# Two decode layers with a resident ring: 64 more places of keys kept between layers, longer loads for heads 27 to 30, W2's last 64 rows loaded apart

## The chip, the cores and the metric

The kernel runs on one core of one Trainium2 chip. The metric is the device time of one execution in microseconds; the median of a kernel's runs is compared.

## What is computed

One token is decoded through two layers that share all weights and caches. Attention has 32 heads over a cache of 8192 keys and values of 128 numbers each, all in float32; then comes a block with a ReLU between two products.

```python
def _A_ref(x, k_cache, v_cache, wq, wo):      # B, Sq = 1, 1; D = 640; H, Dh = 32, 128; Sk = 8192
    q = (x @ wq).reshape(B, Sq, H, Dh).transpose(0, 2, 1, 3)
    scores = jnp.einsum("bhqd,bhkd->bhqk", q, k_cache) * (Dh ** -0.5)
    p = _softmax(scores, axis=-1)
    o = jnp.einsum("bhqk,bhkd->bhqd", p, v_cache)
    return o.transpose(0, 2, 1, 3).reshape(B, Sq, H * Dh) @ wo
...
x = x + _A_ref(_layernorm(x, axis=-1), A_k_cache, A_v_cache, A_wq, A_wo)
x = x + _B_ref(_layernorm(x, axis=-1), B_w1, B_w2)      # relu(x @ w1) @ w2, Dff = 1728
x = x + _A_ref(_layernorm(x, axis=-1), A_k_cache, A_v_cache, A_wq, A_wo)
x = x + _B_ref(_layernorm(x, axis=-1), B_w1, B_w2)
```

A head's keys are 4 MB and its values 4 MB, so a layer's caches are 256 MB, far more than fits beside the engines. Nearly all of the time is the reading of these.

## The kernel before

**The ring.** One SBUF tile, `ring`, takes the caches as they stream in. It is counted in places: one place is 8 numbers on each of 128 partitions, 4096 B. It has `RING` = 4760 places, `KEPT` = 3960 and 800 more. A head's keys take 1024 places, and so do its values. `UNITS` says in which blocks a head lies in DRAM; heads up to 26 are one block of keys and values (the host lays the caches out in the order of use, each block as 128 long rows), heads 27 to 31 are cut finer. A piece of keys is (row group, first column, columns); n columns of keys take n/2 places. A piece of values is (block, first row, rows).

**Two layers, one pass back.** Layer 0 walks heads 0 to 31, layer 1 walks them backwards, since both use the same cache. The last units of layer 0, those of heads 29 to 31 from `DROPPED` on, stay in the ring, `KEPT` places in all, and layer 1 doesn't load them again. Two units of head 30 go to the tiles `wct` and `mix` for layer 1 (`load_beside`, L227).

**What sets the order of loads.** `todo` is a fixed list of loads for the whole program. `pump` (L207) takes from its head: it looks for free places in one run (`place`, L181, for loads without a fixed place; a fixed one for heads 2 to 26, in slots of 256 places) and issues the load on SP's queue (L221); where there is no room it stops, and nothing behind it in the list is issued. `release` frees the places of a piece when PE's matmuls on it are written, and calls `pump` again. So on the chip SP waits for PE's use of a piece, then issues the load that takes its place. At the end of a layer four loads of W2 (12 blocks of 640 numbers) go to the 800 places behind `KEPT` and to what PE has freed.

**Beside it.** ScalarE's queue issues the loads of Wq and Wo in pairs (`load_pair`, L271), of W1 (L797), of W2's last two blocks (`w2_rest`, L799: 128 x 1280 numbers, in the tile `w_t`; of the second block only 64 rows are not zero) and of a piece of the weights for `mixing` (L802). `due` (L783) starts these by the head that is worked on.

**One head.** `scores` (L494) multiplies the keys in the ring by a spread-out query on PE (L499). DVE takes the maxima (L510), ScalarE the exponentials (L524), DVE transposes (L528), and `values` (L548) multiplies the values in the ring (L554). `output` brings the parts together. The two columns of a head's state for the softmax lie in the tile `h_t`, its sum in `sums`. The queries of four heads are computed ahead by a generator that PE and DVE work off in turns; `queries_by_halves` yields between DVE's write of `q_row` (L433) and PE's matmuls on it (L439), so that PE may do other work there. `mixing` uses the constant `ident`, a 128 x 128 identity that POOL makes once at the start. The program works on constants, Wq, Wo and the ring in SBUF; `dynamic_dma_scratch_size` reserves more of it.

Of the kernel before, what the change touches and what calls it, by code (L numbers as in the profile page):

```python
# [43 lines left out]
PARTS = {(0, 0): [4, 9], (1, 26): [4, 8], (1, 25): [4, 8], (1, 2): [4, 8], (1, 1): [2, 4, 6, 8], (1, 0): [2, 4, 6, 7, 8, 9]}  # L44
# [19 lines left out]
DROPPED = {29: 9, 30: 2}  # L64
KEPT = 3960
# [40 lines left out]
def decode_kernel(ctx: ExitStack, tc: tile.TileContext, x, kv, wqo, w1, w2, w2_rest, out):  # L106
# [16 lines left out]
    apart = {(29, 9): (3800, KEPT), (30, 0): (4464, 4544), (30, 1): (4544, RING), (30, 2): (3072, 3800)}  # L123
# [3 lines left out]
    def all_of(layer, u):  # L127
        todo.append((layer, u, 0, len(UNITS[u[0]][u[1]][1]), None))
# [8 lines left out]
    def turning(layer, heads, slot):  # L137

        for h in heads:
            for a, end in parts_of(layer, h):  # L140
                while a < end:
                    b = min(end, a + SLOTS - slot)
                    todo.append((layer, (h, 0), a, b, SLOT * slot))
                    slot = (slot + b - a) % SLOTS
                    a = b

    def anywhere(layer, h):
        for a, b in parts_of(layer, h):
            todo.append((layer, (h, 0), a, b, None))
# [22 lines left out]
    for us, dram in ((order, kv), (W2_ALL, w2)):
        o = 0
        for u in us:
            n = 8 * P * size(UNITS[u[0]][u[1]])
            source[u] = dram[o : o + n].rearrange("(p m) -> p m", p=P)
            o += n
# [29 lines left out]
    def pump():  # L207
        while todo:
            layer, u, first, last, at = todo[0]
            unit = UNITS[u[0]][u[1]]  # L210
            ns = [wide(kind_of(unit, t), piece) for t, piece in enumerate(unit[1])]
            n = sum(ns[first:last])
            if at is None:
                at = place(layer, u, n)
# [5 lines left out]
            o = 8 * sum(ns[:first])  # L220
            nc.sync.dma_start(ring[:, 8 * at : 8 * (at + n)], source[u][:, o : o + 8 * n])  # L221
            for t in range(first, last):
                live[layer, u, t] = at, ns[t]
                at_of[layer, u, t] = ring, 8 * at
                at += ns[t]

    def load_beside(where, at, n):  # L227
# [3 lines left out]
        nc.sync.dma_start(where[:, at : at + n], source[u])  # L231
# [136 lines left out]
    def deviations(xt, s):  # L368
# [4 lines left out]
        xc = work.tile([P, 2 * DH], F32, name="q_row")[:, :DR]  # L373
# [22 lines left out]
    def queries(g, xc, r):  # L396
# [12 lines left out]
        row = work.tile([P, 2 * DH], F32, name="q_row")[:, :DH]  # L409
# [8 lines left out]
    def queries_by_halves(g, xc, r):  # L418
# [696 lines left out]
```

## Time and profile before

| | |
|---|---|
| median of 3 runs | 1349.29 us (1348.77 to 1350.27) |
| profiled execution, its own time | 1349.0 us |
| its span | 1347.2 us |
| PE busy | 797.8 us (59%) |
| DVE busy | 248.3 us (18%) |
| ScalarE busy | 58.5 us (4%) |
| POOL busy | 2.9 us |
| read from HBM | 573.65 MB, 426 GB/s over the span |

The span is what the profiler's records cover; 1.8 us of the execution's own time lie around it. The lines below name L-numbers of the kernel before. A DMA's name reads destination<-source; `SPq` and `ACTq` are the queues that SyncE and ScalarE issue. "PE ps L499 <- DMA ring<-in_kv" is a wait of PE for a load of the ring.

### The profile page before, as it was taken

The numbers are of one execution on the slowest core, as the hardware profiler recorded it, in microseconds if no ns is written. First come the engines' busy times: TensorE is split into PE (matmuls) and PEld (weight loads), VectorE is DVE, ScalarE is ACT, GpSimd is POOL, SyncE is SP. The second block draws the span as 40 slices with busy tenths as digits, with TensorE's granted clock in tenths as the row PEclk, the third lists the DMA queues.
The fourth block names the chain that finished last, engine by engine and source line by source line (L and its number), as shares of the span: only waits on it lengthen the run. The fifth ranks groups of instructions, "written<-read, shape, count | busy, mean of one in ns | idle before, by whom it ended". The sixth has DMA issues, their size and how long they took to land.

```text
span 1347.2 us, 13344 instructions
## 1 busy us (share of the span) xinstructions
PE 797.8 (59%) x5966; PEld 261.2 (19%) x5966; DVE 248.3 (18%) x774; ACT 58.5 (4%) x149; POOL 2.9 (0%) x10
## 2 busy tenths in 40 slices
PE   3564445563655664667688754455466654656667
PEld 1121111111211211112252211112121111211214
DVE  1121111121212121112122211122111121111212
ACT  0000000000000000000000000000000000000000
POOL 0000000000000000000000000000000000000000
PEclk9688777778977886788798777898778788878889
DMA  9999999999999999999999999999999999999997
GB/s 413 429 427 437 430 439 428 438 420 428 442 434 422 441 427 423 446 419 419 425 385 425 435 432 436 424 441 429 437 430 430 424 437 436 434 419 438 424 426 326
DMA packets 22673, 574.52 MB, mean 426 GB/s; under 512 B 2516, under 2 KB 2648, under 8 KB 5464
## 3 DMA queue, kind: packets, MB, share of 16 engines
q1 hardware_dynamic: 19592, 529.84, 91.6%
q10 hardware_dynamic: 3024, 43.83, 7.7%
q8 instruction: 47, 0.77, 0.2%
q14 instruction: 10, 0.08, 0.0%
HBM read 573.65 MB, written 0.00 MB: 426 GB/s over the span
## 4 chain that ended last, share of the span: by engine, by line
DMA 65%; PE 26%; DVE 5%; ACT 1%; issue 1%; another core or an unknown queue 1%; ACTq 0%; SPq 0%; DVEq 0%
DMA ring<-in_kv 65%; PE ps L499 13%; PE outs L554 7%; DVE h_t L510 2%; ACT p L524 1%; DVE pt L528 1%; PE pm L515 1%; PE acc L468 1%; PE px L424 1%; DVE p L591 1%; PE px L456 0%; PE px L675 0%; DMA ring<-in_w 0%; DVE pT L530 0%
## 5 line engine op out<-in xcount | busy, mean ns | idle before, releaser
L499 PE MATMUL ps<-ring,spread_q 128*32 128x512 f32 (+3 forms) x2104 | 324.3, 765 | 312.2 <-DMA ring<-in_kv 307.3
L554 PE MATMUL outs<-ring,pT 128*4 128x512 f32 (+1 forms) x2032 | 258.9, 648 | 48.4 <-DVE pT L530 24.4
L499 PEld LDWEIGHTS ps<-ring,spread_q 128*32 128x32 f32 x2104 | 78.2, 137 | 493.2 <-issue 338.5
L510 DVE TENSOR_REDUCE h_t<-ps 128x1 f32<-128x512 f32 x64 | 44.3, 692 | 611.1 <-PE ps L499 611.1
L524 ACT ACTIVATE p<-ps,h_t 128x512 f32<-128x512 f32 x64 | 44.0, 687 | 1223.2 <-DVE h_t L522 1223.2
L554 PEld LDWEIGHTS outs<-ring,pT 128*4 128x4 f32 x2032 | 51.3, 91 | 211.0 <-issue 172.8
L601 PE MATMUL pm<-ones,p 128*128 128x1 f32 x120 | 22.9, 260 | 95.0 <-DVE p L591 95.0
L587 DVE TENSOR_SCALAR p<-outs,ind 128x128 f32<-128x128 f32 x60 | 21.1, 351 | 269.0 <-PE outs L554 269.0
L591 DVE SCALAR_TENSOR_TENSOR p<-outs,ind,p 128x128 f32<-128x128 f32 x180 | 63.1, 351 | 6.4
L528 DVE STREAM_TRANSPOSE pt<-p 128x512 f32<-128x512 f32 x64 | 46.5, 727 | 58.4 <-ACT p L524 58.4
L515 PE MATMUL pm<-row_of,h_t 128*128 128x16 f32 x128 | 26.3, 281 | 49.6 <-DVE h_t L510 48.9
L601 PEld LDWEIGHTS pm<-ones,p 128*128 128x128 f32 x120 | 17.8, 188 | 151.5 <-DVE p L591 150.2
L515 PEld LDWEIGHTS pm<-row_of,h_t 128*128 128x128 f32 x128 | 20.0, 196 | 109.8 <-DVE h_t L510 108.0
L675 PE MATMUL px<-w_t,wct 128*128 128x448 f32 (+1 forms) x80 | 36.7, 574 | 1.0 <-ACT wct L668 1.0
L424 PE MATMUL px<-pair,ln_xc 128*32 128x256 f32 x280 | 34.6, 396 | 4.4 <-ACT mix L683 4.4
L468 PE MATMUL acc<-pair,o_cols 128*32 128x320 f32 x224 | 36.2, 469 | 0.0
L424 PEld LDWEIGHTS px<-pair,ln_xc 128*32 128x32 f32 x280 | 15.7, 113 | 21.4 <-ACT mix L683 8.5
L522 DVE TENSOR_REDUCE h_t<-pm 128x1 f32<-128x16 f32 x64 | 11.2, 175 | 33.0 <-PE pm L515 33.0
L468 PEld LDWEIGHTS acc<-pair,o_cols 128*32 128x32 f32 x224 | 12.9, 117 | 16.8 <-issue 15.7
L675 PEld LDWEIGHTS px<-w_t,wct 128*128 128x128 f32 x80 | 13.8, 197 | 10.8 <-issue 9.3
L530 DVE COPY pT<-pt 128x64 f32<-128x64 f32 x64 | 14.4, 224 | 2.2
L605 DVE COPY o_cols<-pm 128x1 f32<-128x1 f32 x56 | 8.9, 159 | 28.4 <-PE pm L601 28.4
(130 smaller groups left out, 212.1 us busy)
## 6 DMA issues: line engine op xcount, KB each, us to landing
ring<-in_kv SPq DMA_DIRECT2D x24, 4096.0 KB, 31.1
ring<-in_kv SPq DMA_DIRECT2D x11, 6144.0 KB, 36.1
ring<-in_kv SPq DMA_DIRECT2D x31, 2048.0 KB, 35.1
pair<-in_wqo ACTq DMA_DIRECT2D x13, 2560.0 KB, 25.8
ring<-in_kv SPq DMA_DIRECT2D x14, 1024.0 KB, 15.1
ring<-in_w SPq DMA_DIRECT2D x4, 1280.0 KB, 25.9
w_t<-in_w ACTq DMA_DIRECT2D x1, 4320.0 KB, 27.5
pair<-in_wqo ACTq DMA_DIRECT2D x3, 1280.0 KB, 13.1
```

Source lines behind the costliest of these rows:

```text
L424: nc.tensor.matmul(pq[32 * j : 32 * j + 32, :n], xc[:, c : c + 1].to_broadcast([P, 32]), wq_t[g][:, c, j * n : (j + 1) * n], start=(c == 0 ...
L468: nc.tensor.matmul(acc[32 * half : 32 * half + 32, : 2 * DR], col.to_broadcast([P, 32]), wt[:, 2 * half * DR : 2 * (half + 1) * DR], start ...
L499: nc.tensor.matmul(hd.ps[32 * g : 32 * g + 32, c : c + n], spread_q[:, 3 - r : 35 - r], tile_of[:, at + g * n : at + (g + 1) * n], start=f ...
L510: nc.vector.tensor_reduce(hd.nm, hd.ps, AX.X, ALU.max, negate=True)
L515: nc.tensor.matmul(pt[:, :16], hd.nm.to_broadcast([P, P]), row_of.rearrange("p g r -> p (g r)"), start=True, stop=True,)
L524: nc.scalar.activation(hd.p, hd.ps, AF.Exp, bias=hd.low, scale=1.0, accum_out=hd.l)
L528: nc.vector.transpose(pt, hd.p)
L554: nc.tensor.matmul(hd.out[32 * g : 32 * g + 4, r : r + m].rearrange("p r d -> p (r d)"), hd.pT[:, 4 * i : 4 * i + 4], tile_of[:, v : v + m ...
L587: nc.vector.tensor_scalar(oc[:, 0], hd.out[:, 0], ind[:, :1], 0.0, op0=ALU.mult, op1=ALU.add)
L591: nc.vector.scalar_tensor_tensor(oc[:, r], hd.out[:, r], ind[:, r : r + 1], oc[:, r - 1], op0=ALU.mult, op1=ALU.add,)
L601: nc.tensor.matmul(pt[:, :1], oc[:, 3], ones, start=True, stop=True)
L675: nc.tensor.matmul(pt[:, :n], wct[:, c], w1_t[:, c, f : f + n], start=(c == 0), stop=(c == NB - 1),)
```

## The change

- **Kept keys.** `KEPT` goes from 3960 to 4024: of head 29's keys 448 columns of the last row group are kept, not 320. Layer 1 loads 64 places less.
- **Room for them.** DMA scratch goes from 1024 to 16. `ident` moves into the ring, behind the slots, so that `make_identity` runs again in layer 1 at the tenth head. The row of `queries_by_halves` moves to the tile "p", and the `yield` between its write and PE's matmuls goes, so `q_row` shrinks. `h_t` goes into `sums`; `ones`, `mhalf`, `ind` and `sel` become one tile; `m_s` shares a tile with `ln_m`.
- **Longer loads.** An entry of `todo` may now join several units (`ENDS` for layer 0, `STARTS` for layer 1), and the units of a head lie in one block in DRAM, so that a load may run over them. SP has 118 DMAs instead of 137: 11 ring loads fewer in layer 0 and 8 fewer in layer 1.
- **W2's rest.** `w2_rest` holds one block (128 x 640). The 64 rows of the second come by eight loads of 8 rows x 640 (`w2_last`), on ScalarE's queue, one at each of the heads 16 to 23 of layer 0; load i goes to every fourth partition from `LAST_AT[i]`.

```diff
-PARTS = {(0, 0): [4, 9], (1, 26): [4, 8], (1, 25): [4, 8], (1, 2): [4, 8], (1, 1): [2, 4, 6, 8], (1, 0): [2, 4, 6, 7, 8, 9]}
+PARTS = {(0, 0): [4, 9], (1, 26): [4, 8], (1, 25): [4, 8], (1, 2): [4, 8], (1, 1): [4, 8], (1, 0): [2, 4, 6, 7, 8, 9]}
...
 UNITS[29] = [
     ("k", K_ALL[:1]),
     ("k", K_ALL[1:2]),
     ("k", [(2, 0, 256)]),
-    ("k", [(2, 256, 256), (3, 128, 64)]),
+    ("k", [(2, 256, 256), (3, 0, 64)]),
     ("v", V_ALL[:1]),
     ("v", V_ALL[1:2]),
-    ("k", [(3, 0, 128)]),
     ("v", V_ALL[2:3]),
     ("v", V_ALL[3:]),
-    ("k", [(3, 192, 320)]),
+    ("k", [(3, 64, 448)]),
...
-DROPPED = {29: 9, 30: 2}
-KEPT = 3960
+DROPPED = {29: 8, 30: 2}
+ROWS = [[(h, i) for i in range(len(UNITS[h]))] for h in range(29)]
+ROWS += [[(h, i) for i in range(len(UNITS[h]))] for h in (29, 30, 31)]
+ENDS = [
+    [(27, 0), (27, 1)],
+    [(28, 0), (28, 1)],
+    [(28, 2), (28, 3)],
+    ROWS[29][:4],
+    [(29, 8)],
+    ROWS[29][4:8],
+    [(30, 0), (30, 1)],
+    [(30, 2)],
+    [(30, 3)],
+    [(30, 4)],
+] + [[u] for u in ROWS[31]]
+STARTS = [
+    [(29, 0)],
+    [(29, 1)],
+    [(29, 2)],
+    [(29, 3)],
+    ROWS[29][4:8],
+    ROWS[28][:3],
+    [(28, 3)],
+    [(27, 0)],
+    [(27, 1)],
+]
+KEPT = 4024
...
+LAST_AT = [32 * half + i for half in range(2) for i in range(4)]
...
-    apart = {(29, 9): (3800, KEPT), (30, 0): (4464, 4544), (30, 1): (4544, RING), (30, 2): (3072, 3800)}
+    apart = {(29, 8): (3800, KEPT), (30, 0): (RING - 296, RING), (30, 2): (3072, 3800)}
...
-    def all_of(layer, u):
-        todo.append((layer, u, 0, len(UNITS[u[0]][u[1]][1]), None))
+    def all_of(layer, us):
+        todo.append((layer, [(u, t) for u in us for t in range(len(UNITS[u[0]][u[1]][1]))], None))
...
-    for h in range(FULL[-1] + 1, H):
-        for i in range(len(UNITS[h])):
-            all_of(0, (h, i))
-    for u in W2_ALL:
-        all_of(0, u)
-    for h in range(H)[:FULL[-1]:-1]:
-        if h != 30:
-            for i in range(len(UNITS[h])):
-                if (h, i) not in kept:
-                    all_of(1, (h, i))
+    for us in ENDS + [[u] for u in W2_ALL]:
+        all_of(0, us)
+    for us in STARTS:
+        all_of(1, us)
...
-            layer, u, first, last, at = todo[0]
-            unit = UNITS[u[0]][u[1]]
-            ns = [wide(kind_of(unit, t), piece) for t, piece in enumerate(unit[1])]
-            n = sum(ns[first:last])
+            layer, pieces, at = todo[0]
+            ns = []
+            for u, t in pieces:
+                unit = UNITS[u[0]][u[1]]
+                ns.append(wide(kind_of(unit, t), unit[1][t]))
+            n = sum(ns)
             if at is None:
-                at = place(layer, u, n)
+                at = place(layer, pieces[0][0], n)
                 if at is None:
                     return
             elif not is_free(at, n):
                 return
             todo.pop(0)
-            o = 8 * sum(ns[:first])
-            nc.sync.dma_start(ring[:, 8 * at : 8 * (at + n)], source[u][:, o : o + 8 * n])
-            for t in range(first, last):
-                live[layer, u, t] = at, ns[t]
+            u, t = pieces[0]
+            block, o = source[u]
+            unit = UNITS[u[0]][u[1]]
+            o += 8 * sum(wide(kind_of(unit, i), unit[1][i]) for i in range(t))
+            nc.sync.dma_start(ring[:, 8 * at : 8 * (at + n)], block[:, o : o + 8 * n])
+            for (u, t), m in zip(pieces, ns):
+                live[layer, u, t] = at, m
                 at_of[layer, u, t] = ring, 8 * at
-                at += ns[t]
+                at += m
...
+    small = consts.tile([P, 12], F32, name="small")
+    ones, mhalf, ind, sel = small[:, 0:1], small[:, 1:2], small[:, 2:7], small[:, 7:12]
...
-    ident = consts.tile([P, P], F32, name="ident")
+    ident = ring[:, 8 * SLOT * SLOTS : 8 * SLOT * SLOTS + P]
     make_identity(nc, ident)
...
-        row = work.tile([P, n], F32, name="q_row")
+        row = work.tile([P, RUN], F32, name="p")[:, :n]
         nc.vector.tensor_scalar(
             row[:64], pq[:64, :n], r[0][:64], SCALE, op0=ALU.mult, op1=ALU.mult
         )
-        yield "pe"
         pt = ps_m.tile([P, 512], F32, name="px")
...
         def __init__(self, h, sums, j):
             self.h = h
             self.ps = ps_s.tile([P, RUN], F32, name="ps")
-            t = work.tile([P, 4], F32, name="h_t", bufs=2)
-            self.nm, self.low = (t[:, i : i + 1] for i in range(2))
-            self.sums = sums
-            self.l, self.rl = sums[:, j : j + 1], sums[:, HG + j : HG + j + 1]
+            self.l, self.rl, self.nm, self.low = (
+                sums[:, HG * i + j : HG * i + j + 1] for i in range(4)
+            )
...
             if L == 0 and where == 4:
                 nc.scalar.dma_start(w1_t, w1)
             if L == 0 and where == 7:
-                nc.scalar.dma_start(w2_t, w2_rest)
+                nc.scalar.dma_start(w2_t[:, 0], w2_rest)
+            if L == 0 and 16 <= where < 24:
+                a = LAST_AT[where - 16]
+                nc.scalar.dma_start(w2_t[a : a + 32 : 4, 1], w2_last[where - 16])
             if where == 8:
                 of, nth = divmod(last, HG)
                 nc.scalar.dma_start(
                     mix[:, :D], wqo[chain(of, 1)][:, of, nth * D : (nth + 1) * D]
                 )
+            if L and where == 9:
+                make_identity(nc, ident)
             if where == 11:
                 slow.append([mixing(), "dve"])
...
-        "w2_rest": rows[:, 4 * F_TILES :],
+        "w2_rest": rows[:, 4 * F_TILES],
+        "w2_last": np.stack([rows[a : a + 32 : 4, 4 * F_TILES + 1] for a in LAST_AT]),
...
-        "TRN2", target_bir_lowering=False, num_devices=1, dynamic_dma_scratch_size=1024
+        "TRN2", target_bir_lowering=False, num_devices=1, dynamic_dma_scratch_size=16
```

The loads that SP issues at the end of layer 0, from heads 25 and 26 (one load each) to head 29 (a row's size is partitions x numbers; a head's keys or values are 8192 numbers), before:

```order
L221 DMA ring<-in_kv 128x16384 x2
L221 DMA ring<-in_kv 128x8192 x2
L221 DMA ring<-in_kv 128x4096 x4
L221 DMA ring<-in_kv 128x2048 x2
L221 DMA ring<-in_kv 128x1024
L221 DMA ring<-in_kv 128x1280
L221 DMA ring<-in_kv 128x2048 x2
L221 DMA ring<-in_kv 128x512
L221 DMA ring<-in_kv 128x2048 x2
L221 DMA ring<-in_kv 128x1280
```

And now, from the same place, up to the first loads of head 30:

```order
L253 DMA ring<-in_kv 128x16384 x3
L253 DMA ring<-in_kv 128x8192 x2
L253 DMA ring<-in_kv 128x6400
L253 DMA ring<-in_kv 128x1792
L253 DMA ring<-in_kv 128x8192
L253 DMA ring<-in_kv 128x2368
L253 DMA ring<-in_kv 128x5824
```

Head 27 is one load instead of two, head 28 two instead of four, head 29 three instead of ten (its kept keys, 1792, ahead of its values), and head 30's first two units one.

The loads that SP issues at the start of layer 1, behind those to `wct` and `mix` (the first are head 29's keys and values, then come heads 28 and 27), before:

```order
L231 DMA mix<-in_kv 128x1728
L221 DMA ring<-in_kv 128x2048 x2
L221 DMA ring<-in_kv 128x1024
L221 DMA ring<-in_kv 128x1280
L221 DMA ring<-in_kv 128x2048 x2
L221 DMA ring<-in_kv 128x512
L221 DMA ring<-in_kv 128x2048 x2
L221 DMA ring<-in_kv 128x4096 x4
L221 DMA ring<-in_kv 128x8192 x6
```

And now:

```order
L264 DMA mix<-in_kv 128x1728
L253 DMA ring<-in_kv 128x2048 x2
L253 DMA ring<-in_kv 128x1024
L253 DMA ring<-in_kv 128x1280
L253 DMA ring<-in_kv 128x8192
L253 DMA ring<-in_kv 128x12288
L253 DMA ring<-in_kv 128x4096
L253 DMA ring<-in_kv 128x8192 x6
```

Head 29's values are one load of 1024 places where they were four of 256, the 512 of keys are gone since they are kept, and head 28 is two loads instead of four.

## Rows read from the trace of the kernel before

**Rows 1.** The page: DMA busy share in tenths and GB/s, 40 slices.

```profile
DMA  9999999999999999999999999999999999999997
GB/s 413 429 427 437 430 439 428 438 420 428 442 434 422 441 427 423 446 419 419 425 385 425 435 432 436 424 441 429 437 430 430 424 437 436 434 419 438 424 426 326
```

**Rows 2.** The page: chain that ended last, share of the span by engine.

```profile
DMA 65%; PE 26%; DVE 5%; ACT 1%; issue 1%; another core or an unknown queue 1%; ACTq 0%; SPq 0%; DVEq 0%
```

**Rows 3.** Waits: who for whom: us in all, count, mean us.

```profile
ACT p L524 <- DVE h_t L522: 1223.2, 64, 41.1
...
PE ps L499 <- DMA ring<-in_kv: 307.3, 48, 18.9
...
PEld px L439 <- DVE q_row L433: 8.3, 8, 1.1
```

**Rows 4.** Timeline of SP at the boundary: start us, us, queue, line, load.

```profile
676.22 0.33 SPq L221 DMA_DIRECT2D ring<-in_w  x1
...
702.30 0.33 SPq L221 DMA_DIRECT2D ring<-in_kv  x1
...
711.08 0.33 SPq L221 DMA_DIRECT2D ring<-in_kv  x1
```

**Rows 5.** Issues at 676.22, 702.30 and 166.52: KB, us to landing.

```profile
ring<-in_w SPq DMA_DIRECT2D x1, 640.0 KB, 22.6
...
ring<-in_kv SPq DMA_DIRECT2D x1, 640.0 KB, 13.6
...
w_t<-in_w_rest ACTq DMA_DIRECT2D x1, 640.0 KB, 24.7
```

**Rows 6.** Windows at both layers' ends: busy by engine, PEclk, DMA share, GB/s.

```profile
694.00:696.00 2.00, 1.90 (x30) 1.29 (x30) 0.97 (x5) 0.37 (x2) 0.00 (x0) 1.00 0.53 225
696.50:697.50 1.00, 1.00 (x34) 0.98 (x37) 0.22 (x2) 0.00 (x0) 0.00 (x0) 1.00 0.41 169
1338.00:1340.00 2.00, 2.00 (x56) 1.66 (x57) 0.53 (x4) 0.00 (x0) 0.00 (x0) 1.00 0.57 238
```

**Rows 7.** The page, DMA queues: packets, MB, share of 16 engines' span.

```profile
q1 hardware_dynamic: 19592, 529.84, 91.6%
...
q8 instruction: 47, 0.77, 0.2%
```

**Rows 8.** Windows of two stretches without idle DMA: columns as in rows 6.

```profile
40.00:600.00 560.00, 310.09 (x2070) 93.76 (x2074) 95.58 (x282) 22.82 (x58) 0.00 (x0) 0.79 1.00 432
610.00:660.00 50.00, 31.57 (x218) 9.90 (x222) 9.62 (x31) 2.33 (x6) 0.00 (x0) 0.76 1.01 423
```

**Rows 9.** DMA packets of 40 to 600, 610 to 660, and from 1344 on.

```profile
DMA packets 6501, 241.64 MB, mean 432 GB/s; under 512 B 720, under 2 KB 720, under 8 KB 976
...
DMA packets 2513, 21.14 MB, mean 423 GB/s; under 512 B 278, under 2 KB 278, under 8 KB 1046
...
DMA packets 8, 0.00 MB, mean 1 GB/s; under 512 B 4, under 2 KB 8, under 8 KB 8
```

**Rows 10.** Timeline: two issues of loads, W2's rest and the output.

```profile
166.52 0.34 ACTq L799 DMA_DIRECT2D w_t<-in_w_rest  x1
...
1344.59 0.66 SPq L1030 DMA_DIRECT2D out<-xr  x1
```

**Rows 11.** Groups by line: POOL's identity: count, busy us, mean ns.

```profile
masks.py:199 POOL TENSOR_SCALAR_AFFINE_SELECT ident<-ident 128x128 f32<-128x128 f32 x1 | 0.3, 292 | 0.1
masks.py:197 POOL MEMSET ident<- 128x128 f32 x1 | 0.2, 204 | 0.3 <-POOLq L1097 0.3
```

**Rows 12.** Chain of waits in time, at the boundary: start us, us, work.

```profile
696.55 4.90 DMA ring<-in_w
...
707.43 3.71 PE ps L499 x32
```

More of the change, by code (lines that the diff above doesn't have):

```diff
@@ L105, in decode_kernel @@
 @with_exitstack
-def decode_kernel(ctx: ExitStack, tc: tile.TileContext, x, kv, wqo, w1, w2, w2_rest, out):
+def decode_kernel(ctx: ExitStack, tc: tile.TileContext, x, kv, wqo, w1, w2, w2_rest, w2_last, out):
     nc = tc.nc
@@ L142, in turning @@
                     b = min(end, a + SLOTS - slot)
-                    todo.append((layer, (h, 0), a, b, SLOT * slot))
+                    todo.append((layer, [((h, 0), t) for t in range(a, b)], SLOT * slot))
                     slot = (slot + b - a) % SLOTS
@@ L148, in anywhere @@
         for a, b in parts_of(layer, h):
-            todo.append((layer, (h, 0), a, b, None))
+            todo.append((layer, [((h, 0), t) for t in range(a, b)], None))
     for h in range(FULL[0]):
@@ L169, in decode_kernel @@
     for u in W2_ALL:
-        all_of(1, u)
+        all_of(1, [u])
     source = {}
[L172 to L177, printed above, removed]
+    o = 0
+    for row in ROWS:
+        n = 8 * sum(size(UNITS[h][i]) for h, i in row)
+        block = kv[o : o + P * n].rearrange("(p m) -> p m", p=P)
+        o += P * n
+        a = 0
+        for h, i in row:
+            source[h, i] = block, a
+            a += 8 * size(UNITS[h][i])
+    o = 0
+    for u in W2_ALL:
+        n = 8 * P * size(UNITS[u[0]][u[1]])
+        source[u] = w2[o : o + n].rearrange("(p m) -> p m", p=P), 0
+        o += n
     live = {}
@@ L230, in load_beside @@
         assert 8 * size(UNITS[u[0]][u[1]]) == n
-        nc.sync.dma_start(where[:, at : at + n], source[u])
+        block, o = source[u]
+        nc.sync.dma_start(where[:, at : at + n], block[:, o : o + n])
         for t, piece in enumerate(pieces):
@@ L288, in decode_kernel @@
     pump()
-    ones = consts.tile([P, 1], F32, name="ones")
+    small = consts.tile([P, 12], F32, name="small")
+    ones, mhalf, ind, sel = small[:, 0:1], small[:, 1:2], small[:, 2:7], small[:, 7:12]
     nc.vector.memset(ones, 1.0)
-    sel = consts.tile([P, 5], F32, name="sel")
     nc.vector.memset(sel, 0.0)
@@ L372, in deviations @@
         nc.vector.tensor_scalar(m, pt[:, :1], 1.0 / D, 0.0, op0=ALU.mult, op1=ALU.add)
-        xc = work.tile([P, 2 * DH], F32, name="q_row")[:, :DR]
+        xc = work.tile([P, DR], F32, name="q_row")
         nc.vector.tensor_scalar(xc, xt, m, 0.0, op0=ALU.subtract, op1=ALU.add)
@@ L408, in queries @@
         yield "dve"
-        row = work.tile([P, 2 * DH], F32, name="q_row")[:, :DH]
+        row = work.tile([P, DR], F32, name="q_row")[:, :DH]
         nc.vector.tensor_scalar(row, pq[:, :DH], r[0], SCALE, op0=ALU.mult, op1=ALU.mult)
@@ L545, in totals @@
         nc.tensor.matmul(pt[:, :HG], ind[:, 4:5].to_broadcast([P, P]), sums[:, :HG], start=True, stop=True)
-        nc.vector.reciprocal(sums[:, HG:], pt[:, :HG])
+        nc.vector.reciprocal(sums[:, HG : 2 * HG], pt[:, :HG])
     def values(hd, piece, where, first, last):
@@ L645, in mixing @@
         wc = mix[:, :D]
-        s = work.tile([P, 1], F32, name="m_s")
+        s = work.tile([P, 1], F32, name="ln_m")
         nc.vector.tensor_reduce(s, wc, AX.X, ALU.add)
@@ L788, in due @@
                 o_cols[k] = work.tile([P, HG], F32, name="o_cols", bufs=2)
-                sums[k] = work.tile([P, 2 * HG], F32, name="sums", bufs=2)
+                sums[k] = work.tile([P, 4 * HG], F32, name="sums", bufs=2)
             if where and j == 0:
@@ L886, in attention_and_mlp @@
                 if k < NG - 1 and j == HG - 1:
-                    nc.vector.tensor_tensor(o_cols[k], o_cols[k], sums[k][:, HG:], op=ALU.mult)
+                    nc.vector.tensor_tensor(o_cols[k], o_cols[k], sums[k][:, HG : 2 * HG], op=ALU.mult)
         hd = opened(H - 1)
@@ L919, in attention_and_mlp @@
                 sums_of_rows(pt, rows, False)
-        o_late = work.tile([P, 2 * DH], F32, name="q_row")[:, :DH]
+        o_late = work.tile([P, DR], F32, name="q_row")[:, :DH]
         nc.vector.tensor_copy(o_late, late)
@@ L1056, in _laid_out @@
     o = 0
-    for h in range(H):
-        for unit in UNITS[h]:
-            n = 8 * size(unit)
-            block = kv[o : o + P * n].reshape(P, n)
-            o += P * n
-            a = 0
+    for row in ROWS:
+        n = 8 * sum(size(UNITS[h][i]) for h, i in row)
+        block = kv[o : o + P * n].reshape(P, n)
+        o += P * n
+        a = 0
+        for h, i in row:
+            unit = UNITS[h][i]
             for t, piece in enumerate(unit[1]):
```

2 lines of the change are left out of this document (removed).

## The prediction, made before the changed kernel ran

> **What bounds the kernel now.** I read the slices first: the DMA engines stand at 9 in 39 of 40 slices and move 413 to 446 GB/s, except in the slice that holds the layer boundary (385) and in the last (326) [rows 1]. The chain of waits gives 65% of the span to DMA [rows 2]. PE waits 307.3 us for ring loads in 48 waits, and ScalarE 1223.2 us for DVE, so neither is short of time [rows 3]. The queue of loads is the bound: what it no longer carries comes off the end, unless it runs dry, and what an engine off that path gets or loses costs nothing.
>
> Not all 16 DMA engines are equally late. The last W2 load of layer 0 is issued at 676.22 and lands after 22.6 us, at 698.8, but from 694 to 696 the DMA share is already 0.53, and 0.41 from 696.5 to 697.5: about half of the engines have run out while the others work on [rows 4 to 6]. Layer 1 ends alike, with 0.57 from 1338 to 1340 [rows 6]. The queue of instruction fetches may be why: 47 packets, 0.2% of 16 engines' span, is 0.002 x 16 x 1347 = 43 engine-us; if they all sat on eight engines, those would lose 5.4 us a run, 2.7 a layer, which is about the lag seen [rows 7]. So a byte saved counts only if it is saved on the late half, and a byte added to the early half is free up to some 3 us a layer.
>
> **The price of bytes and packets.** Two stretches in which the engines are never idle differ in packet size: 40 to 600 moves 241.64 MB in 6501 packets, 610 to 660 moves 21.14 MB in 2513 [rows 8, 9]. With a price a per MB and b per packet, in engine-us: 560 x 16 = 8960 = 241.64a + 6501b and 50 x 16 = 800 = 21.14a + 2513b. This gives a = 36.86 us (2.304 us of all sixteen engines) and b = 8.3 ns. With the share as printed in the second (1.01 for 50 us, so 808) b is 12.4 ns; that is my upper end, and 0 the lower. I take 8.3 because it comes with full engines in both. In the first stretch 720 of the 6501 packets are under 512 B, which leaves 8.0 larger ones to each small one: a load of 128 rows is eight data packets and one small one on every engine, nine in all [rows 9].
>
> **The change part by part.**
> - *64 more places kept.* A place is 32 B on each of 128 partitions, 4096 B; 64 are 0.2621 MB less to read in layer 1, on all engines alike: 0.2621 x 2.304 = **-0.60 us**.
> - *Longer loads.* SP issues 19 ring loads fewer: 11 at the end of layer 0 (head 27 one, 28 two, 29 seven, 30 one), 8 in layer 1 (29 four, 28 two, head 1 two). 19 x 9 x 8.3 ns = **-1.42 us** on each engine (-2.12 at 12.4 ns).
> - *W2's rest.* The load on ScalarE's queue drops from 640 to 320 KB [rows 5], 0.3277 MB: x 2.304 = **-0.75 us** on each engine. Its 64 true rows come back as eight loads of eight rows, 20 KB each, 0.1638 MB. No load of eight rows is in the trace. The nearest row is the output's: four rows, and eight packets in that stretch, four of them under 512 B, so four engines with one data and one small packet each, not sixteen [rows 9]. I therefore take one row per engine on eight engines. Each of the eight gets 0.0205 MB x 36.86 = 0.755 us and 16 packets x 8.3 ns = 0.13 us, **+0.89 us**; the other eight get nothing.
>
> The page "DMA: Bandwidth & Descriptors" of the Trainium skill, section "Why a DMA increments its semaphore by 16 and not by 1", speaks against this last edit: the number of engines is the largest up to 16 that divides the slowest dimension, and on the hardware queues they are always the lowest-numbered. By it 64 rows in one load would be spread over sixteen engines, and eight loads of eight rows all fall on the same eight; the output's eight packets agree. By it the edit saves 0.75 us on eight engines and costs 0.14 us on the other eight, where one load of 64 rows (0.0102 MB x 36.86 + 5 x 8.3 ns = 0.42 us on each engine, an estimate from that page) would have saved 0.34 us on all. The page does not say whether the eight are the late ones, and no row here does.
>
> So an engine that gets no W2 rows is relieved by 0.60 + 1.42 + 0.75 = 2.78 us (unrounded terms), and one that gets them by 2.78 - 0.89 = 1.89 us. From the profiled run, 1349.0: 1346.2 or 1347.1. The median shown is 1349.29, 0.29 above the profiled run, so on the median's footing 1346.5 or 1347.4.
>
> **Edits that I cost at nothing, and their cover.** The queries' row: PE now waits in place for DVE's row instead of passing to other work. A wait of this kind costs 8.3 us in eight in the trace, 1.1 each [rows 3]; some 14 are 15 us, beside 307.3 us of waiting for loads. Without that cover, at the boundary, one is 1.1 us. The identity: it now lies in ring places, so it is rebuilt once in layer 1, by POOL in 0.2 + 0.3 us [rows 11] at the tenth head; ring loads over these places wait for its readers, the mixing steps two heads later, and SP's later loads stand behind such a load. The queue ahead is long (22.6 us from issue to landing [rows 5]), so a wait up to about that is hidden; more would show in full. ScalarE's queue issues eight more loads at 0.34 to 0.66 us [rows 10], beside 1223.2 us of idle time. Softmax's two small columns in `sums`, the joined constants and `ln_m` change no duration. The ring's base moves in SBUF by 992 B per partition; no row shows loads at another offset. A gain is excluded, since the bytes and packets stay; the loss has no bound here except that 1% on the rate would be 13 us. I take 0, as one set of rows and lengths is written either way.
>
> **The rivals.**
> *A, the forecast:* the eight rows per load go to the early half. The late half is relieved by 2.78 us: **1346.5**. For it: the early engines have 3 us of idle time at the boundary, and 0.89 fits into it. Against it: no row names an engine.
> *B:* they go to the late half, which gets 1.89 us: **1347.4**. A partly overlapping set ends here too, as one late engine is enough. For it: one of the two halves must be hit.
> *C, what it says is not done on the wire:* joining loads saves no engine time, because a small packet overlaps the data of the next load; only bytes count, -0.60 - 0.75 = -1.36 (unrounded): 1349.29 - 1.36 = **1347.9**. For it: b comes from one mix of packet sizes, and small data packets may carry the cost rather than their number. Against it: at 0 ns the second stretch would have had to take 21.14 x 37.08 = 784 of its 800 engine-us.
> *D, slower:* the queue runs dry at the start of layer 1. Head 29's values, four loads of 1 MB, become one of 4 MB, which needs 1024 places in one run; these are free when head 31's last keys are scored. Before, the first of the four was issued at 711.08, as PE's scores ended at 707.43 + 3.71 = 711.14; the load ahead of it, issued at 702.30, lands at 702.30 + 13.6 = 715.9 [rows 4, 5, 12]. With about 1 us from issue to the first packet the cover is 715.9 - 711.1 - 1.0 = 3.8 us. It decides if PE frees the places later than that. PE's granted clock is 1.00 (2.4 GHz) there, against 0.76 to 0.79 in the stretches where it waits for loads [rows 6, 8]; should PE stand still longer at the boundary, at a wait for a query row or for W2, and be granted 1.2 GHz after it, the 711.1 - 701.4 = 9.7 us from the load that ends the boundary (696.55 + 4.90, [rows 12]) to the last key piece become 19.4. Then the queue is dry for 9.7 - 3.8 = 5.9 us: 1346.5 + 5.9 = **1352.4**. Against it: PE runs without long waits there, and the same pieces free the same places as before.
>
> **How the numbers follow.** A measurement of this kernel tells about 0.2% from no change, 2.70 us: faster is under 1346.59, slower over 1351.99. A 0.56, B 0.22, C 0.13, D 0.09. A's center is just under the bound, so the sign hangs on tenths: b between 8.3 and 12.4 ns takes A to 1345.8, and the runs of before themselves spread from 1348.77 to 1350.27. Of A 0.34 falls under the bound and 0.22 over it; of B 0.05 falls under, by the higher b; C none. Faster 0.39, same 0.52, slower 0.09. The forecast is A's 1346.5. The range goes from 1345.2 (A at 12.4 ns, less half a microsecond of spread) to 1348.6 (C and as much above it, for a part of the merges lost); D is left out.
>
> **What would show it.** HBM read should fall from 573.65 by 0.43 MB to 573.2; The last load should land about 2.8 us earlier and the tail after it stay as long. At the boundary the idle share of the early half between 694 and 697 should shrink in A and grow in none; in B the lag between first and last engines grows by 0.9 us in layer 0. In C the loads of heads 28 to 30 land as late as their bytes say. In D there is a dip of the DMA share right after 712 and a PEclk below 1.00 from 698 to 711. The prediction is wrong if the rate between 40 and 600 is no longer 432 GB/s, or if a load joined from several waits for places after the queue ahead of it has run out.

## The result: slower by 0.16%, outside the range

The changed kernel takes 1351.4 us (21 runs, 1349.19 to 1355.55), the kernel before 1349.56 beside it; the ratio is 1.0016, 95% interval 1.0009 to 1.0022. The forecast was 1346.5 and the range ended at 1348.6. By the bound of 0.2% this is "same", but its sign is the other one, and its runs spread over 6.4 us where those of before spread over 1.5. (A ratio is estimated from all runs and is not quite the quotient of two medians.) The profiled execution is one of 1352.54 us with a span of 1350.8.

The page after, to set beside [rows 1, 2, 7, 9]:

```profile
DMA  9999999999999999999999999999999999999997
GB/s 412 428 426 437 438 428 433 433 423 433 438 434 421 439 439 422 434 429 394 425 366 429 433 435 436 424 442 426 440 435 425 423 437 432 432 419 442 423 428 311
DMA packets 20064, 574.07 MB, mean 425 GB/s; under 512 B 2276, under 2 KB 2408, under 8 KB 4520
HBM read 573.23 MB, written 0.00 MB: 424 GB/s over the span
DMA 63%; PE 28%; DVE 5%; ACT 1%; issue 1%; another core or an unknown queue 1%; ACTq 0%; SPq 0%; DVEq 0%
```

The change does what it says: 0.42 MB less is read, with 20064 packets where there were 22673. But slice 19 (608 to 642 us) has fallen from 419 to 394 GB/s, the boundary to 366, the last slice to 311, and 2% of the span has gone from DMA to PE. The windows name the places (columns as in [rows 6]); first the kernel before, then after:

```profile
610.00:615.00 5.00, 3.01 (x28) 1.21 (x32) 1.44 (x6) 0.78 (x2) 0.00 (x0) 1.00 0.99 423
625.00:630.00 5.00, 2.49 (x16) 0.96 (x16) 1.97 (x6) 0.78 (x2) 0.00 (x0) 0.79 1.00 421
696.00:698.00 2.00, 2.00 (x60) 1.48 (x56) 0.44 (x4) 0.00 (x0) 0.00 (x0) 1.00 0.53 195
698.00:700.00 2.00, 2.00 (x42) 1.18 (x42) 0.91 (x6) 0.00 (x0) 0.00 (x0) 1.00 1.02 374
```

```profile
610.00:615.00 5.00, 4.26 (x28) 1.00 (x20) 0.67 (x1) 0.00 (x0) 0.00 (x0) 0.71 0.81 344
625.00:630.00 5.00, 4.36 (x22) 1.73 (x24) 0.87 (x4) 0.00 (x0) 0.00 (x0) 0.66 0.83 273
698.00:700.00 2.00, 2.00 (x40) 1.66 (x44) 0.65 (x5) 0.30 (x2) 0.00 (x0) 1.00 0.06 26
700.00:702.00 2.00, 2.00 (x50) 1.25 (x39) 0.48 (x4) 0.00 (x0) 0.00 (x0) 1.00 0.66 172
```

**The queue runs dry at the end of layer 0**, where head 28 is loaded, and for longer at the boundary, as PE is late there: by the shares from 690 to 706 the engines stand idle for some 3 us, before for 2. The chain of after shows why PE is late (start us, us, work), and SP's timeline what waits for it:

```profile
608.93 5.38 PE ps L528 x32
614.33 0.70 DVE sums L539
```

```profile
592.99 0.33 SPq L253 DMA_DIRECT2D ring<-in_kv  x1
...
614.33 0.33 SPq L253 DMA_DIRECT2D ring<-in_kv  x1
```

Head 27 comes as one load, and PE scores nothing of it until the last byte lands, at 608.9. Before, its keys had landed at 599.1 on their own, and PE scored them once it was through with head 26:

```profile
605.10 1.06 PE L499 MATMUL ps<-ring,spread_q 128*32 128x512 f32 x8
...
606.62 2.78 PE L499 MATMUL ps<-ring,spread_q 128*32 128x512 f32 x24
```

So the scores start 3.8 us later, and they also take longer: 5.4 us instead of 4.3 with its pause, at a granted clock of 0.71 from 610 to 615. They end 4.9 us later. The next load after 592.99, a joined one of 1024 places, is issued at 614.33, as these scores end. Before, head 28 came in four loads of 512 places, issued at 578.48, 592.01, 607.75 and 609.47.

**The tail is longer too.** Before, the last ring load of values was issued at 1303.90 and landed 29.5 us later, at 1333.4, and the output was issued at 1344.59 [rows 10], 11.2 us after that. After, in the timeline and in the list of issues:

```profile
1299.32 0.33 SPq L253 DMA_DIRECT2D ring<-in_kv  x1
...
1348.06 0.66 SPq L1064 DMA_DIRECT2D out<-xr  x1
```

```profile
ring<-in_kv SPq DMA_DIRECT2D x1, 512.0 KB, 36.2
```

It lands at 1335.5, and the output follows 12.6 us after it. I had written that the tail would stay as long.

### The profile page after: what moved, and what is told of

It is laid out like the page before. It is cut to its first block, busy times and chain, and to the rows that moved or that the text cites. A ratio compares the mean times of both kernels' runs of the same rounds, so it can differ in the third digit from the quotient of the medians.

```text
span 1350.8 us, 13296 instructions
## 1 busy us (share of the span) xinstructions
PE 804.9 (60%) x5950; PEld 262.5 (19%) x5950; DVE 247.9 (18%) x774; ACT 58.5 (4%) x149; POOL 3.4 (0%) x12
## 2 busy tenths in 40 slices
DMA packets 20064, 574.07 MB, mean 425 GB/s; under 512 B 2276, under 2 KB 2408, under 8 KB 4520
## 4 chain that ended last, share of the span: by engine, by line
DMA 63%; PE 28%; DVE 5%; ACT 1%; issue 1%; another core or an unknown queue 1%; ACTq 0%; SPq 0%; DVEq 0%
DMA ring<-in_kv 63%; PE ps L528 13%; PE outs L583 8%; DVE sums L539 2%; DVE pt L557 1%; ACT p L553 1%; PE acc L498 1%; PE pm L544 1%; DVE p L620 1%; PE px L486 1%; PE px L455 1%; DVE pT L559 0%; PE acc L719 0%; DVE sums L551 0%
## 5 line engine op out<-in xcount | busy, mean ns | idle before, releaser
L528 PE MATMUL ps<-ring,spread_q 128*32 128x512 f32 (+4 forms) x2088 | 325.8, 774 | 304.9 <-DMA ring<-in_kv 301.7
L539 DVE TENSOR_REDUCE sums<-ps 128x1 f32<-128x512 f32 x64 | 44.2, 691 | 599.3 <-PE ps L528 599.3
L553 ACT ACTIVATE p<-ps,sums 128x512 f32<-128x512 f32 x64 | 44.0, 687 | 1225.2 <-DVE sums L551 1225.2
L630 PE MATMUL pm<-small,p 128*128 128x1 f32 x120 | 23.2, 262 | 94.9 <-DVE p L620 94.9
L616 DVE TENSOR_SCALAR p<-outs,small 128x128 f32<-128x128 f32 x60 | 21.0, 351 | 275.5 <-PE outs L583 275.5
L620 DVE SCALAR_TENSOR_TENSOR p<-outs,small,p 128x128 f32<-128x128 f32 x180 | 63.1, 351 | 6.4
L544 PE MATMUL pm<-row_of,sums 128*128 128x16 f32 x128 | 25.7, 276 | 49.7 <-DVE sums L539 48.9
L630 PEld LDWEIGHTS pm<-small,p 128*128 128x128 f32 x120 | 18.1, 190 | 152.3 <-DVE p L620 149.9
L544 PEld LDWEIGHTS pm<-row_of,sums 128*128 128x128 f32 x128 | 19.4, 191 | 108.3 <-DVE sums L539 106.6
L551 DVE TENSOR_REDUCE sums<-pm 128x1 f32<-128x16 f32 x64 | 11.2, 175 | 32.4 <-PE pm L544 32.4
```

Of the source, the lines that this page charges most:

```text
L528: nc.tensor.matmul(hd.ps[32 * g : 32 * g + 32, c : c + n], spread_q[:, 3 - r : 35 - r], tile_of[:, at + g * n : at + (g + 1) * n], start=f ...
L539: nc.vector.tensor_reduce(hd.nm, hd.ps, AX.X, ALU.max, negate=True)
L544: nc.tensor.matmul(pt[:, :16], hd.nm.to_broadcast([P, P]), row_of.rearrange("p g r -> p (g r)"), start=True, stop=True,)
L553: nc.scalar.activation(hd.p, hd.ps, AF.Exp, bias=hd.low, scale=1.0, accum_out=hd.l)
L616: nc.vector.tensor_scalar(oc[:, 0], hd.out[:, 0], ind[:, :1], 0.0, op0=ALU.mult, op1=ALU.add)
L620: nc.vector.scalar_tensor_tensor(oc[:, r], hd.out[:, r], ind[:, r : r + 1], oc[:, r - 1], op0=ALU.mult, op1=ALU.add,)
```

## Experiments: which join costs

Theory 1: PE can start on a joined load only when its last byte has landed, so joins cost time at head 27 and at head 1. Theory 2, the rival: the loss sits in the other edits. Each had 9 or 11 runs, beside the kernel before on the same chip (medians 1349.68 to 1350.02); the table at the end of this section has the results. "Tail" is the time from the landing of the last values to the output's issue in the profiled execution.

**Head 27 apart.**

```diff
-    [(27, 0), (27, 1)],
+    [(27, 0)],
+    [(27, 1)],
```

> After with one edit: in layer 0 head 27's keys and values are again two loads, all else as after. Theory 1 (PE has to wait for the last byte of a joined load; head 27's one 8 MB load makes it start 9.7 us later, at 608.93 instead of about 599, so places come free later and the queue runs dry between 610 and 630): 1348.5 to 1349.5, the DMA share between 600 and 630 back at 0.95 to 1.0, and the first half of head 28's keys issued before 600. Theory 2 (the loss against the forecast sits in the other edits: eight loads of eight rows, the ring's new place, the query row's wait): 1351.4 as after.

1351.1, ratio 1.0009: by the ratios 0.9 us below after, where I had expected 2 to 3. The dry stretch is gone, and layer 0's last values land at 689.7 instead of 692.3 (but at 690.3 in the second profiled execution of after, e13 below), yet the end didn't move as far: the tail is 13.6 us, and in this execution the queue ran dry at the start of layer 1 instead. That is taken up below.

**Everything apart**, in both layers, with 27 as above and `PARTS` as before:

```diff
-    [(28, 0), (28, 1)],
-    [(28, 2), (28, 3)],
+    [(28, 0)],
...
+    [(28, 3)],
...
-    ROWS[29][4:8],
-    ROWS[28][:3],
-    [(28, 3)],
+    *[[u] for u in ROWS[29][4:8]],
+    *[[u] for u in ROWS[28]],
```

> After with all joined loads taken apart again, in both layers and for head 1; the 64 kept places, W2's eight loads and the moved tiles stay. Theory 1: 64 places give -0.60, W2 between -0.75 and +0.13, so 1348.2 to 1349.1 against 1349.56 before. Theory 2: the 19 extra loads cost 1.4 us on top of after, 1352.8. If joining loads is free on the wire: theory 2 gives 1351.4.

1349.13, ratio 0.9994, tail 11.2. Theory 2 is out: without the joins the other edits cost nothing that the runs can tell.

**Head 27's join alone**, on the kernel with everything apart:

> All loads apart but head 27's keys and values in layer 0, which are one load: the one suspected join alone. Theory 1: 2 to 3 us above the run with all apart, with PE's first scores of head 27 some 9 us later and a dip of the DMA share behind it. Theory 2: within 0.1 us of the run with all apart.

1348.98: it costs nothing. So my first reading was wrong in part: one late head is covered as long as head 28's halves are loads of their own, which find 512 places earlier (the DMA share from 610 to 615 is 1.00, after 0.88 from 605 to 610). The long dry stretch needs both, 27 in one load and 28 in loads of 1024 places.

**Head 1 as before**, all else as after:

```diff
-(1, 1): [4, 8]
+(1, 1): [2, 4, 6, 8]
```

> After with head 1's load of layer 1 in four parts again instead of two. Theory 1 says that the same thing happens once more at the end of layer 1, where the last values land at 1335.48 and the end comes 15.3 us later instead of 13.8 as before: 1349.9 with a tail of 13.8 us, or 1350.8 if head 0's smaller parts already let PE catch up half. Theory 2: 1351.5, 0.15 above after for the two more loads.

1349.59, ratio 0.9997, tail 11.2: theory 1 as expected, and the largest part. From here on theory 1b: a join costs where PE or a place is short, and saves its packets elsewhere.

**Head 1's join alone**, on everything apart:

> All loads apart but head 1's two pairs of parts at the end of layer 1: that join alone. Theory 1b (PE starts on a pair only when its last byte lands and is behind at the end): the tail from the last values' landing to the output's issue is 12.6 to 13.6 us instead of 11.2, and the time 1.2 to 2.3 above the 1349.1 of all apart. Theory 2: 1349.0.

1351.91, tail 13.5: two joins that save 18 packets on each engine put 2.0 us (by the ratios) to 2.5 us (by the medians against before) on the kernel with everything apart. The tails agree: 11.2 to 11.3 us in all eleven profiled executions with head 1 apart, 12.3 to 14.7 in the seven with a join there.

**Its halves.** On the kernel with heads 27 and 1 apart, the keys joined in one run, the values in the next:

```diff
-(1, 1): [2, 4, 6, 8]
+(1, 1): [4, 6, 8]
...
-(1, 1): [2, 4, 6, 8]
+(1, 1): [2, 4, 8]
```

> The run with heads 27 and 1 apart (1348.3), but with head 1's two key parts joined and its two value parts apart. If the tail is late because the values' matmuls and the work queued behind them start only when the whole 4 MB of values has landed, keys alone cost nothing: tail 11.2, 1348.3. If any late start of PE on head 1 is enough, the keys cost half or more: tail 12.3 to 13.5, 1349.5 to 1350.8.

> The mirror of the run before: head 1's values joined, its keys apart. By the values' theory the tail is 12.6 to 13.6 and the time 1349.7 to 1350.8, as with both joined; by the other it is as the run before.

Keys joined 1350.39 with a tail of 12.3, values joined 1351.78 with one of 14.7: either late start is enough, and the values' is worse than expected. PE's timeline shows it (start us, us, line, work, idle before), first with head 1 apart (e7 in the table), then with its values joined, there with a window too:

```profile
1307.31 1.90 PE L584 MATMUL outs<-ring,pT 128*4 128x512 f32 x16 [0.64 <-DVE pT L560]
...
1321.60 1.92 PE L529 MATMUL ps<-ring,spread_q 128*32 128x512 f32 x16 [1.29 <-DMA ring<-in_kv]
```

```profile
1313.01 3.45 PE L584 MATMUL outs<-ring,pT 128*4 128x512 f32 x16 [5.16 <-DMA ring<-in_kv]
...
1326.16 1.93 PE L529 MATMUL ps<-ring,spread_q 128*32 128x512 f32 x16
```

```profile
1310.00:1315.00 5.00, 1.99 (x12) 0.45 (x16) 0.00 (x0) 0.00 (x0) 0.00 (x0) 0.50 1.01 429
```

Apart, PE catches up and waits for head 0's last keys (1.29 us); they bound it. Joined, PE stands for 5.2 us, runs the first values at a granted clock of 0.50 (1.2 GHz), and comes to head 0's last keys 3.5 us after they have landed (they did at 1322.66); that delay goes straight to the end.

**How much of it is the clock?** Values joined, and four more filler matmuls (two records each in the profile) on PE while it would stand:

```diff
-                keep_busy(1)
+                keep_busy(5 if L and where == H - 2 else 1)
```

> The run with head 1's values joined (tail 14.7 us, 1351.8), with four more idle-time matmuls of 512 columns, 1.1 us each, put on PE between head 1's exponentials and its values in layer 1, where it stands 5.2 us waiting for the joined load. If the late landing alone makes the tail (the clock theory is wrong), tail and time stay: 14.7 and 1351.8. If the halved clock after the wait (0.50 from 1310 to 1315, 3.45 us for sixteen matmuls instead of 1.90) is part of it, the first values take 1.90 and the tail falls to 12.9 to 13.3, the time to 1350 to 1350.3.

1350.15, tail 13.2. PE's timeline and the same window:

```profile
1314.11 1.90 PE L584 MATMUL outs<-ring,pT 128*4 128x512 f32 x16 [0.87 <-DMA ring<-in_kv]
```

```profile
1310.00:1315.00 5.00, 4.01 (x20) 1.26 (x22) 0.24 (x2) 0.00 (x0) 0.00 (x0) 1.00 0.98 416
```

Of the 3.5 us on the tail 1.5 are the clock that fell while PE stood, 2.0 the late landing, by one execution each. The ratios, 1.0013 and 1.0006, put the clock at 0.9 us, with intervals that overlap.

**Which joins are worth having.** Heads 27 and 1 apart, the other joins as after; then also `STARTS` apart:

> After with head 27 and head 1 apart, but the joined loads of heads 29 and 28 at the start of layer 1 kept. Against the first run of this series it tells what these joins do alone. Theory 1b (the 1024-place load is issued at about 713.7 whenever layer 0 ends, since it waits for the last key piece of head 31, and by then an earlier queue has run out): 1.3 to 2.4 us slower than the first run, 1349.3 to 1350.4, with idle DMA engines between 700 and 720. Theory 2: 0.45 faster, for six loads fewer.

> After with three places taken apart: head 27 in layer 0, heads 29 and 28 at the start of layer 1, head 1 at its end. The joins of heads 28 to 30 at the end of layer 0 stay. Theory 1b (a join costs where PE or a place is short: the stretch 600 to 640, the start of layer 1 and the tail; elsewhere it saves its packets): the DMA engines idle no longer at 600 to 640 nor at 700 to 720, the tail is 11.2 us, and against before it gains 0.8 to 1.0 in layer 0 and 0.6 in layer 1: 1347.7 to 1348.3. Theory 2 (joins don't matter, the other edits cost): 1349 to 1351.

1348.32 and 1348.58; the first is the fastest kernel here, 0.13% below before (interval 0.04 to 0.22). It and after once more, on one chip:

> The changed kernel once more, beside the next run on one chip: 1351.4 to 1351.8 if the sum of its three costs stands (head 1's join 2.3 to 2.6, head 27's joined with 28's 1 to 1.4, the boundary's spread), and 2.5 to 3.5 us above the next run.

> The kernel with only heads 27 and 1 apart, once more: 1348.3 to 1348.7, 1.2 to 1.7 us below before. If it comes out at 1349.5 or above, the earlier result was a lucky set of runs.

1351.61 and 1348.86 (0.08% below before, interval -0.01 to 0.17): after is 2.75 us above the same kernel without these two joins. The start of layer 1, which I had expected to cost 1.3 us or more with joins, cost nothing in these runs; in the profiled executions with head 27 alone apart (e1) and with head 1 alone apart (e4) it did. The difference is PE's clock. The execution of e1 first, windows and timeline, then the one with 27 and 1 apart (e7):

```profile
703.00:708.00 5.00, 4.54 (x52) 3.43 (x55) 1.21 (x7) 0.00 (x0) 0.55 (x1) 0.50 1.00 416
708.00:714.00 6.00, 5.67 (x32) 1.17 (x32) 0.25 (x1) 0.00 (x0) 0.00 (x0) 0.65 0.84 345
```

```profile
707.93 5.75 PE L529 MATMUL ps<-ring,spread_q 128*32 128x512 f32 x32 [0.46 <-DVE spread_q L519]
...
713.75 0.33 SPq L254 DMA_DIRECT2D ring<-in_kv  x1
```

```profile
708.00:714.00 6.00, 5.11 (x66) 1.67 (x62) 1.79 (x5) 0.78 (x2) 0.00 (x0) 1.00 1.08 450
```

```profile
706.22 3.64 PE L529 MATMUL ps<-ring,spread_q 128*32 128x512 f32 x32 [0.46 <-DVE spread_q L519]
...
709.92 0.33 SPq L254 DMA_DIRECT2D ring<-in_kv  x1
```

At 0.50 the scores of head 31 take 5.75 us instead of 3.64, the 1024-place load is issued at 713.75, and the DMA share falls to 0.84. In e4 it is the same:

```profile
708.45 5.67 PE L528 MATMUL ps<-ring,spread_q 128*32 128x512 f32 x32 [0.46 <-DVE spread_q L518]
...
714.19 0.33 SPq L253 DMA_DIRECT2D ring<-in_kv  x1
```

This is rival D's mechanism. It shows in two of the ten profiled executions with these joins and after's kept places, and e1 and e7 run the same code up to there.

**The other terms.** 64 places kept less, with `STARTS` joined and with `STARTS` apart:

```diff
-    ("k", [(2, 256, 256), (3, 0, 64)]),
+    ("k", [(2, 256, 256), (3, 0, 192)]),
...
-    ("k", [(3, 64, 448)]),
+    ("k", [(3, 192, 320)]),
...
-KEPT = 4024
+KEPT = 3960
```

> The run with heads 27 and 1 apart (1348.3), with the old 3960 places kept: the first term alone undone. 0.2621 MB more in layer 1 at 2.304 us per MB is 0.60 us: 1348.9. Theory against it: the places taken from the 800 others make SP wait more, so that nothing was gained by them: 1348.3.

> The run with three places apart (1348.6), with the old 3960 places kept: the first term alone, without the joined loads at the start of layer 1 that made the queue run dry there when fewer places were kept. 0.2621 MB at 2.304 us per MB: 0.60 us, 1349.2, with no idle engines from 700 to 720. If the kept places' worth is mostly the room that they leave, 1350 or more.

1353.60 and 1349.06, where the first was expected at 1348.9. With `STARTS` apart the 64 places are worth 0.5 us by the medians and 1.3 by the ratios, each uncertain by more than a microsecond; the sum's 0.60 fits. With `STARTS` joined they are worth 5 us: with 64 places less no run of 1024 is free until PE is through part of head 31's values. The load that went out at 709.92 now goes at 716.80, and the DMA share falls to 0.38:

```profile
716.80 0.33 SPq L254 DMA_DIRECT2D ring<-in_kv  x1
```

```profile
714.00:718.00 4.00, 4.00 (x64) 1.32 (x56) 0.93 (x3) 0.00 (x0) 0.00 (x0) 1.00 0.38 115
```

W2's rest whole again, at head 7 and without the eight loads (on the kernel with 27 and 1 apart), and then its 64 rows as one load (on the one with `STARTS` apart as well):

```diff
-                nc.scalar.dma_start(w2_t[:, 0], w2_rest)
+                nc.scalar.dma_start(w2_t, w2_rest)
...
-            if L == 0 and 16 <= where < 24:
-                a = LAST_AT[where - 16]
-                nc.scalar.dma_start(w2_t[a : a + 32 : 4, 1], w2_last[where - 16])
+            if L == 0 and where == 16:
+                nc.scalar.dma_start(w2_t[:64, 1], w2_last)
```

> The run with heads 27 and 1 apart (1348.3), with W2's rest loaded whole as before the change (640 KB, zeros and all) and no loads of eight rows. By the terms as measured from landing times (0.74 us off every engine, 0.40 back on the mean engine, 0.9 on those that get rows) the mean engine is 0.34 later at the end of layer 0 and the time between 0.15 faster and 0.75 slower: 1348.2 to 1349.1. If eight short loads disturb the ring's loads, it is faster by more than 0.3.

> The run before this (three joins apart), with W2's last 64 rows in one load instead of eight of eight rows. If eight rows go to eight engines, five of them early and three late as the landing times of the run with all apart suggest, then one load over sixteen engines costs each of them 0.42 us where the late three had 0.89: 0.2 to 0.5 us faster than the run before, with the lag between first and last engine smaller. If the eight rows all fall on early engines: 0.4 slower. Under 0.2 neither is told apart by the time, and the landing times decide.

Whole: 1349.35, 0.5 us above one set of runs of the kernel with the edit and 1.0 above the other, so the edit seems to pay a little; the intervals don't tell it from nothing. One load: 1349.96, 1.4 us slower than eight (e5; the intervals overlap), where I had expected 0.2 to 0.5 faster or 0.4 slower. Over 360 to 374, one load first, eight (of which one falls there) second:

```profile
360.00:374.00 14.00, 3.39 (x32) 0.84 (x22) 1.72 (x6) 0.00 (x0) 0.00 (x0) 0.73 0.96 387
```

```profile
360.00:374.00 14.00, 3.68 (x34) 0.93 (x26) 1.75 (x7) 0.00 (x0) 0.00 (x0) 0.78 1.00 433
```

Of the forecasts not yet named, e5, e11 and e14 came out 0.2 to 0.3 us above their ranges.

| run | edit | us | ratio to before (95%) | tail |
|---|---|---|---|---|
| after | | 1351.4 | 1.0016 (1.0009 to 1.0022) | 12.6 |
| e13 | after again | 1351.61 | 1.0015 (1.0006 to 1.0023) | 13.2 |
| e1 | 27 apart | 1351.1 | 1.0009 (1.0000 to 1.0018) | 13.6 |
| e4 | 1 apart | 1349.59 | 0.9997 (0.9988 to 1.0006) | 11.2 |
| e7, e14 | 27 and 1 apart | 1348.32, 1348.86 | 0.9987 (0.9978 to 0.9996), 0.9992 (0.9983 to 1.0001) | 11.2 |
| e5 | 27, 1, starts apart | 1348.58 | 0.9988 (0.9979 to 0.9997) | 11.2 |
| e2 | all apart | 1349.13 | 0.9994 (0.9985 to 1.0003) | 11.2 |
| e3 | only 27 joined | 1348.98 | 0.9993 (0.9984 to 1.0002) | 11.3 |
| e8 | only 1 joined | 1351.91 | 1.0009 (1.0000 to 1.0018) | 13.5 |
| e9, e10 | e7, 1's keys / values joined | 1350.39, 1351.78 | 0.9998, 1.0013 (0.0009 each way) | 12.3, 14.7 |
| e15 | e10, PE kept busy | 1350.15 | 1.0006 (0.9996 to 1.0015) | 13.2 |
| e12, e16 | e7, e5 with 64 places less | 1353.60, 1349.06 | 1.0026, 0.9998 (0.0009 each way) | 11.2 |
| e11 | e7, W2's rest whole | 1349.35 | 0.9997 (0.9988 to 1.0006) | 11.3 |
| e6 | e5, W2's rows in one load | 1349.96 | 0.9998 (0.9989 to 1.0007) | 11.2 |

## Why the prediction was wrong, point by point

**The prices held, in most executions.** I compared when the same load lands on the mean of the sixteen engines, from the landing times in the traces. W2's rest: at the load that lands at 350 us, the kernel with 27 and 1 apart is 0.67 us ahead of before, the one with W2's rest whole 0.08 behind: 0.75, as forecast. The eight short loads: back to 0.28 ahead at 542 us, so 0.39 for the mean engine, where 0.89 on eight of sixteen is 0.44. The joins of heads 28 to 30 in layer 0: from 0.28 to 1.01 ahead, 0.73 for ten loads at 0.075. Kept places and joins at layer 1's start: from 0.70 to 1.87 ahead, 1.17, forecast 0.60 + 6 x 0.075 = 1.05. The kept places alone, with all joins apart: from 0.05 behind to 0.60 ahead where the load of 64 places is gone, 0.65, forecast 0.60 + 0.075.

The steps are read in one execution each, and not all of them repeat. W2's rest does: the sixteen executions with that edit are 0.59 to 0.77 ahead of before at 354 us. The joins of heads 28 to 30 gave 0.69 to 0.74 in six of eleven executions with head 27 apart and less in five, down to a loss of 0.20 in e14, the same kernel as e7. The start of layer 1 gave 1.2 to 1.4 in eight of ten; the other two are e1 and e4, with rival D. At the last values e7 is 1.6 us ahead of before and e14 2.3 behind. Against e7 it lost 0.9 us between 542 us and the end of layer 0, 1.7 at the boundary, and 1.2 between 933 and 978 us, where the loads are those of before; why is open.

**Which engines get the eight rows** was the difference between A and B. Neither: from 356 to 543 us the seven parts of a load that land early fell back by 0.58 us against before, the nine late ones by 0.27, as if five of the eight were early and three late. The small packets bear the count out, before and after from 350 to 560:

```profile
DMA packets 2287, 90.86 MB, mean 433 GB/s; under 512 B 242, under 2 KB 242, under 8 KB 242
```

```profile
DMA packets 2420, 90.97 MB, mean 433 GB/s; under 512 B 305, under 2 KB 305, under 8 KB 369
```

64 more of 2 to 8 KB, 63 more under 512 B: eight loads with eight engines each. By the rule of the Trainium skill's page "DMA: Bandwidth & Descriptors" (section "Why a DMA increments its semaphore by 16 and not by 1") it is eight; the trace agrees. The estimate from that page for 64 rows in one load, 0.42 us an engine, failed: the mean engine was 1.35 us later behind it.

**The step that failed is "Longer loads".** It priced a join by the packets that it saves, and took for granted that nobody waits for its first half. Its -1.42 us was right on the wire (as far as it was measured, and in most executions), and what stood against it was never in the sum: PE's later start. At head 1 that is some 2.5 us (after 1.0016, e4 0.9997), at 27 together with 28 another 0.7 to 1.3 (e4 0.9997; e14 0.9992 and e7 0.9987, one kernel; these intervals overlap). The landings bear the second out: on the mean, the last values of layer 0 are 0.5 to 1.9 us behind before in the three executions with 27 and 28 joined (e13, after, e4) and 0.1 to 1.0 ahead in the nine that differ there only by 27 in two loads. Together they turn over 1 us of gain into 2 of loss. I had excluded this with the sentence that the tail after the last load stays as long; what spoke against it stood in the trace of before, where PE waits for the last byte of four of the halves of heads 1 and 0 and works each off before the next lands:

```profile
1303.88 1.93 PE L499 MATMUL ps<-ring,spread_q 128*32 128x512 f32 x16 [0.35 <-DMA ring<-in_kv]
...
1313.67 1.90 PE L554 MATMUL outs<-ring,pT 128*4 128x512 f32 x16 [0.36 <-DMA ring<-in_kv]
...
1318.57 1.06 PE L499 MATMUL ps<-ring,spread_q 128*32 128x512 f32 x8 [0.55 <-DMA ring<-in_kv]
...
1323.46 1.92 PE L499 MATMUL ps<-ring,spread_q 128*32 128x512 f32 x16 [1.29 <-DMA ring<-in_kv]
```

The last of the prediction's signs, a joined load that waits for places after the queue ahead of it has run out, came true at 614.33. (By its own terms the range starts at 1345.3, not 1345.2; nothing hangs on it.)

**Rival D** had the right mechanism: a 1024-place load, PE later at a lower clock, a dry queue. The prediction gave it 9 in 100 at one place, the start of layer 1. There it occurs in some executions only. Whether this makes up the wide spread of after's runs is not shown: neither profiled execution of after has it. The same price, from the same rows, stood unasked at three other joined heads.

**At nothing, rightly:** the query row's wait, the rebuilt identity, the ring's new address, ScalarE's eight issues. With all joins apart these add up to no loss that can be told (0.9994, where kept places and W2 alone come to 0.9992 for the mean engine), and the stretch from 40 to 600 moves 432 GB/s as before.

## What to carry to other kernels

A joined load has two prices: the packets that it saves, on the queue, and the wait for its last byte, on its reader; where the reader is the one that frees the space for later loads, or where little else comes after it, the second is microseconds against hundredths. Before joining, ask of each load who starts on its first half, and how long that reader would stand. Join where the reader is a full load behind anyhow; keep the last loads of a stage short.

## What was not expected of the hardware

- PE stood 5.2 us for the joined values, after that its granted clock was 0.50 from 1310 to 1315, and sixteen matmuls took 3.45 us instead of 1.90. With matmuls in the gap it stayed at 1.00. Here the wait cost more than its own length.
- One 64-row load of 160 KB on ScalarE's queue delayed the ring's loads by 1.35 us on the mean engine, eight loads of eight rows with the same bytes by 0.40 in all. In the trace the ring's 64 KB packets beside the one load took 2.6 us instead of 2.42. Why is open.
